# Attention and two feed-forward layers on one core: six weight tiles converted a stage later, the squares' low parts on GpSimd

## The chip, the cores and the metric

The kernel runs on one NeuronCore of a Trainium2 chip. The metric is the time of one execution on the device, in microseconds. Five engines work side by side, each through its own queue in order: TensorE (matmuls, PE in the profile, its weight loads PEld), VectorE (DVE), ScalarE (ACT), GpSimd (POOL) and SyncE (SP), which here issues the DMAs.

## The reference

The input goes through attention with a mask by blocks of 64, and its output, 2304 tokens of 512, through two feed-forward layers of width 2048. The first one squares the positive part of the hidden values, the second one takes a rational function of them.

```python
attn_out = _attn_ref(**attn_kwargs)          # 4 x 8 heads, 576 tokens, 64 wide
x = attn_out.transpose(0, 2, 1, 3).reshape(B * S, H * D)
h = np.maximum(x @ w_in, 0.0)                # first layer, 512 -> 2048 -> 512
x = h * h @ w_out
h = x @ w_in2                                # second layer
P = a[0] + a[1] * h + a[2] * h2 + a[3] * h3
Q = 1.0 + np.abs(b[0]) * np.abs(h) + np.abs(b[1]) * h2
out = P / (Q + 1e-06) @ w_out2
```

## The kernel before, in words

Every product of the feed-forward layers is made of three matmuls: each operand is kept as a high part, rounded to the format of the matmul, and a low part, the rest. PAIRS lists the three combinations.

The weights come in as 64-bit numbers and are converted on the chip, 16 + 16 tiles (in and out) of 128 by 512 for each layer. Converter does that, a job a tile. `load` keeps 2 or 3 raw tiles on the way (SP's queue, L91); a call of `step` finishes the tile before (ScalarE writes its high part at L108, GpSimd its low part at L109) and begins the next one: ScalarE L115, and four instructions of VectorE, L116, L117, L119 and L120. A raw tile's buffer is free for the next load when its L120 is done. Arguments of the call are gates: instructions behind which those of the step are queued on their engine.

The work has three stages.

- Stage one is attention, with the first half (8 of 16 hidden tiles) of the first layer woven in, sequence by sequence (`moe_a`, names ha, ya, ga and s). Its result goes to memory as yp (from yo, L435). The last sequence's share has no attention beside it: the loop at L565 to L573 advances it in 128 pieces and calls convB, which converts the second half's weights (names bi0 to bi7 and bo0 to bo7).
- Stage two is the second half of the first layer (L602 to L645): five blocks of tokens, 384, 384, 512, 512 and 512 wide, 8 units each, one for each hidden tile. A unit u makes h of its tile (12 matmuls, names hb) and y of the tile two units before (12 matmuls, yb). Between the two, `relu_square` takes the positive part (rb, ScalarE), its square's high part (gb, ScalarE L443), the square on VectorE (sb, L444) and its low part (gb, L445). At a block's end VectorE adds yp and stores the sum to xs2. Weights of the second layer (ci0, co0, ci1, ...) are converted beside it by conv3, into buffers of which the later half is free only when stage two has read its own weights for the last time.
- Stage three is the second layer (names hc, yc, gc, t, wq, ab), five blocks of 16 units.

Inputs of a block are read as x (xb, xc), split into high and low by ScalarE and GpSimd (`split_x`). The order in each queue is made by a scheduler that takes the instructions as the program lists them and moves up what it holds to be ready, except behind gates. The numbers in names: ha3_1_7 is sequence 3, part 1, tile 7; hb4_3 is block 4, tile 3.

The lines that the change touches are the two lists of jobs (L559 and L588), the pace of convB (L566), the condition and the place of the call of conv3 in stage two (L612) and the engine of the square's low part (L624):

```python
    def step(self):
        if self.mid:
            ...
            nc.scalar.activation(w[:, 0, :], c, AF.Copy)
            eng.tensor_tensor(w[:, 1, :], c, f(w[:, 0, :]), op=ALU.subtract)
        if self.raws:
            ...
```

Of the kernel before, what the change touches and what calls it, by code (L numbers as in the profile page):

```python
# [24 lines left out]
NM = DFF // P  # L25
HALF = NM // 2
HS = S // 2
SCALE = 0.125
PLAIN = 10
SUBS = ((0, 320), (320, S))  # L30
# [13 lines left out]
def f(ap):  # L44
    return ap.bitcast(F32)
# [3 lines left out]
def attention_moe_moe(ctx: ExitStack, tc: tile.TileContext, q, k, v, wi1, wo1, wi2, wo2, a, b, out):  # L49
    nc = tc.nc  # L50
# [77 lines left out]
    g1 = tc.alloc_tile_pool(name="g1", bufs=1, side="right")  # L128
# [98 lines left out]
    def emit_s(i):  # L227
# [8 lines left out]
        for t in g:  # L236
# [9 lines left out]
            if t == 4:  # L246
                parts = [(ps[:, 0, 0:HS], 0, HS), (ps[:, 1, 0:HS], HS, S)]
            else:
# [191 lines left out]
    def relu_square(alloc, h, g, nm, eng):  # L440
        r, s = alloc("ab", f"r{nm}"), alloc("w", f"s{nm}")
        nc.scalar.activation(r, h, AF.Relu)  # L442
        done = (nc.scalar.activation(g[:, 0, :], r, AF.Square),  # L443
                nc.vector.tensor_tensor(s, r, r, op=ALU.mult))  # L444
        eng.tensor_tensor(g[:, 1, :], s, f(g[:, 0, :]), op=ALU.subtract)  # L445
        return done

    units = [Head(hd) for hd in range(NH_ALL)]
# [43 lines left out]
    for i in range(NI + 5):  # L492
# [22 lines left out]
        for back in range(4):  # L515
            n = units_at.get(i - back)
# [35 lines left out]
    def split_x(xt, kk, n):  # L552
# [3 lines left out]

    w2 = tc.alloc_tile_pool(name="w2", bufs=1, reuse_waits="tile")
    wB = {}
    convB = Converter(g1, 3, [  # L559
        (f"b{kind}{m}", src[HALF + m], w2, kind, wB, m, nc.gpsimd)  # L560
        for m in range(HALF) for kind, src in (("i", wi1), ("o", wo1))])
    n = 0
    SPLITS = (73, 80, 87, 94)
    x_first = load_x(xs, *blocks2[0], "b0")
    while True:  # L565
        if n % 7 == 0:  # L566
            convB()
        if n in SPLITS:
            split_x(x_first, SPLITS.index(n), blocks2[0][1])
        advance(1)  # L570
        if not moes:
            break
        n += 1  # L573
# [7 lines left out]
    g2 = tc.alloc_tile_pool(name="g2", bufs=1, side="right", reuse_waits="tile")  # L581
    psh = tc.alloc_tile_pool(name="psh", bufs=1, space=PSUM, reuse_waits="tile")

    def tmp(tag, n, nm, dt=F32):
        return g2.tile([P, n], dt, tag=tag, name=nm, bufs={"t": 3, "o": 1}.get(tag, 2), padded_shape=[P, 512])

    w3 = {}
    conv3 = Converter(g2, 2, [  # L588
        (f"c{kind}{m}", src[m], wpool if m < HALF else w2, kind, w3, m, nc.gpsimd)
        for m in range(NM) for kind, src in (("i", wi2), ("o", wo2))])  # L590

# [12 lines left out]
    done = ()  # L604
    acc = {}
    units = [(j, m) for j in range(len(blocks2)) for m in range(HALF)]
# [2 lines left out]
    conv3.load()  # L609
    for u in range(len(units) + LAG):  # L610

        if u % 2 == 0 or u > len(units) - HALF:  # L612
            conv3(*done)
        if u < len(units):
            j, m = units[u]
            t0, n = blocks2[j]
            nxt = (xs, *blocks2[j + 1], f"b{j + 1}") if j + 1 < len(blocks2) else (xs2, *blocks3[0], "c0")
            if m == 0:
                xt[j + 1] = load_x(*nxt)
            elif 2 <= m < 2 + KK:  # L620
                split_x(xt[j + 1], m - 2, nxt[2])
            ps = h_matmul(wB["i", m], xt[j], n, f"b{j}_{m}")
            g = g2.tile([P, 2, 512], F32R, tag="g", name=f"gb{j}_{m}", bufs=3)
            done = relu_square(lambda tag, nm: tmp(tag, n, nm), ps[:, 0:n], g[:, :, 0:n], f"b{j}_{m}", nc.vector)  # L624
            gs[u] = g
        if u >= LAG:
            j, m = units[u - LAG]
            t0, n = blocks2[j]
            g = gs.pop(u - LAG)
            last = m == HALF - 1  # L630
            if m == HALF // 2:
                for c in range(KK):
                    ypart[c] = tmp("t" if c < 3 else "o", n, f"yp{j}_{c}")
                    nc.sync.dma_start(ypart[c], yp[:, c, t0:t0 + n])
            for c in range(KK):
                if m == 0:
                    acc[j, c] = psh.tile([P, 512], F32, tag="y", name=f"yb{j}_{c}", bufs=4)
                for i, (zw, zg) in enumerate(PAIRS):
                    nc.tensor.matmul(acc[j, c][:, 0:n], wB["o", m][:, zw, P * c:P * (c + 1)], g[:, zg, 0:n],  # L639
                                     start=m == 0 and i == 0, stop=last and i == 2)  # L640
            if last:
                for c in range(KK):
                    y = ypart[c]
                    nc.vector.tensor_tensor(y, acc.pop((j, c))[:, 0:n], y, op=ALU.add)
                    nc.sync.dma_start(xs2[:, c, t0:t0 + n], y)  # L645


    units = [(j, m) for j in range(len(blocks3)) for m in range(NM)]
    xt = {0: xt[len(blocks2)]}
    mid, gf = {}, {}  # L650
    for u in range(len(units) + LAG):
        if u - 2 in gf:
            t = gf.pop(u - 2)
            n = blocks3[units[u - 2][0]][1]
            g = g2.tile([P, 2, 512], F32R, tag="g", name=f"gc{u - 2}", bufs=3)
# [13 lines left out]
        if u < len(units):  # L669
            j, m = units[u]  # L670
            t0, n = blocks3[j]
# [5 lines left out]
            ps = h_matmul(w3["i", m], xt[j], n, f"c{j}_{m}")  # L677
# [7 lines left out]
            done = (taken, nc.vector.scalar_tensor_tensor(t, t, a1, h, op0=ALU.add, op1=ALU.mult))  # L685
            mid[u] = (ab, w, t)
        if u >= LAG:
            j, m = units[u - LAG]
            t0, n = blocks3[j]
            g = gs.pop(u - LAG)  # L690
            for c in range(n // P):
# [7 lines left out]
                if m == NM - 1:  # L699
                    if c % 2 == 0:  # L700
                        o = g2.tile([P, 2, DM], F32, tag="wraw", name=f"o{j}_{c}", bufs=2)
# [64 lines left out]
```

## Time and profile before

| | |
|---|---|
| median of three runs | 1058.16 us (1053.28 to 1058.83) |
| the profiled execution | 1054.84 us |
| its span | 1053.1 us |
| TensorE busy | 1015.3 us, 96% |
| VectorE busy | 818.8 us, 78% |
| ScalarE busy | 705.8 us, 67% |
| GpSimd busy | 625.3 us, 59% |
| mean granted clock of TensorE | 0.989 |

The profiled execution took 1.74 us more than its span, and lies 3.3 us under the median. Stage one ends at 440.6 us of the span, stage two at 639.9 us. A busy share is a mean over stages: it is read by stretches, and an engine's wait counts where it is the last thing that TensorE waits for.

### The profile page before, as it was taken

The page shows a single profiled execution, that of the slowest core. Times are in us where ns is not written, and L with a number is a line of the kernel's source. Part 1 is how long each engine was busy: PE and PEld are TensorE (multiplying, and loading weights), DVE is VectorE, ACT ScalarE, POOL GpSimd, SP SyncE. Part 2 cuts the span into 40 slices and gives each one's busy share as a digit, 9 for nine tenths or more (in the row PEclk, how much of TensorE's full clock was granted, in tenths as well). Part 3 has the DMA queues.
Part 4 walks back from the last instruction along what each step waited for, and adds up shares of the span by engine and source line. Part 5 has one row for each costly group of instructions (what it writes and reads, how often), then busy time and mean ns, then how long its engine had stood idle before and what let it go on. Part 6 is the DMA issues. An engine that isn't in the chain of part 4 may idle for free.

```text
span 1053.1 us, 17059 instructions
## 1 busy us (share of the span) xinstructions
PE 1015.3 (96%) x5696; PEld 884.6 (84%) x5696; DVE 818.8 (78%) x1584; ACT 705.8 (67%) x1556; POOL 625.3 (59%) x630
## 2 busy tenths in 40 slices
PE   6999899999999998799999999889999999999997
PEld 3667799999999998799888887667888888899996
DVE  7998877878677759978766889888876766776766
ACT  5787677868777754554443445778877777788875
POOL 4789877867686756733321435568555655655542
PEclk9999999999999999899999999999999999999999
DMA  7664433333323215353524355101100200010000
GB/s 249 193 221 144 132 107 105 95 105 117 115 85 107 65 42 165 114 186 122 170 82 139 106 174 163 58 1 41 41 1 1 71 0 1 31 41 1 30 2 30
DMA packets 53784, 96.11 MB, mean 91 GB/s; under 512 B 12096, under 2 KB 27712, under 8 KB 53696
## 3 DMA queue, kind: packets, MB, share of 16 engines
q1 hardware_dynamic: 53408, 94.72, 28.2%
q8 instruction: 45, 0.74, 0.3%
q14 instruction: 43, 0.35, 0.1%
q10 hardware_dynamic: 288, 0.30, 0.1%
HBM read 72.88 MB, written 18.87 MB: 87 GB/s over the span
## 4 chain that ended last, share of the span: by engine, by line
PE 67%; DVE 18%; POOL 4%; ACT 4%; DMA 3%; issue 3%; SPq 0%; POOLq 0%; DVEq 0%; ACTq 0%
PE yc L697 15%; PE hc L597 14%; PE ya L430 7%; PE hb L597 7%; PE ha L418 6%; PE yb L639 6%; PE tp L316 4%; PE pv L382 4%; PE sy L254 2%; DVE stat L277 2%; PE sx L254 2%; DVE s L444 1%; DVE wq L663 1%; DVE gb L445 1%; DMA raw_ci<-in_wi_dram 1%
## 5 line engine op out<-in xcount | busy, mean ns | idle before, releaser
L697 PE MATMUL yc<-w_co,gc 128*128 128x512 f32 x864 | 211.7, 392 | 7.3 <-ACT gc L656 7.3
L597 PE MATMUL hc<-xc,w_ci 128*128 128x512 f32 (+1 forms) x960 | 211.3, 368 | 3.4 <-DVE t L685 3.4
L597 PEld LDWEIGHTS hc<-xc,w_ci 128*128 128x128 f32 x960 | 175.9, 188 | 30.9 <-DVE t L685 4.7
L697 PEld LDWEIGHTS yc<-w_co,gc 128*128 128x128 f32 x864 | 160.7, 188 | 41.6 <-ACT gc L656 10.0
L657 POOL TENSOR_TENSOR gc<-t,gc 128x512 fp32r<-128x512 f32 (+1 forms) x78 | 106.6, 1372 | 134.0 <-issue 91.0
L301 POOL TENSOR_SCALAR p<-p,stat 64x64 f32<-64x64 f32 (+4 forms) x160 | 103.8, 652 | 62.6 <-DVE stat L297 20.2
L430 PE MATMUL ya<-ga,w_ao 128*128 128x320 f32 (+1 forms) x768 | 119.6, 303 | 5.3 <-POOL ga L445 5.1
L418 PE MATMUL ha<-xt,w_ai 128*128 128x320 f32 (+1 forms) x768 | 120.3, 305 | 3.0 <-ACT yo L435 2.4
L430 PEld LDWEIGHTS ya<-ga,w_ao 128*128 128x128 f32 x768 | 108.3, 193 | 7.3 <-POOL ga L445 6.9
L683 POOL TENSOR_TENSOR wq<-wq,ab 128x512 f32<-128x512 f32 (+1 forms) x78 | 96.3, 1235 | 29.6 <-ACT wq L681 29.2
L418 PEld LDWEIGHTS ha<-xt,w_ai 128*128 128x128 f32 x768 | 109.0, 194 | 5.3 <-ACT yo L435 2.6
L597 PE MATMUL hb<-xb,w_bi 128*128 128x512 f32 (+1 forms) x480 | 106.1, 367 | 0.8 <-ACT yo L435 0.8
L639 PE MATMUL yb<-gb,w_bo 128*128 128x512 f32 (+1 forms) x480 | 106.2, 367 | 0.4 <-DVE gb L445 0.4
L684 DVE TENSOR_TENSOR t<-hc,t 128x512 f32<-128x512 f32 (+1 forms) x80 | 50.9, 637 | 63.3 <-ACT t L682 63.3
L656 ACT ACTIVATE gc<-t 128x512 fp32r<-128x512 f32 (+1 forms) x80 | 47.1, 589 | 76.0 <-DVE t L665 74.2
L639 PEld LDWEIGHTS yb<-gb,w_bo 128*128 128x128 f32 x480 | 87.6, 188 | 12.1 <-DVE gb L445 0.7
L597 PEld LDWEIGHTS hb<-xb,w_bi 128*128 128x128 f32 x480 | 87.4, 188 | 12.2 <-ACT yo L435 1.1
L316 PE MATMUL tp<-ident,p 128*128 128x128 f32 (+1 forms) x480 | 84.0, 283 | 4.8 <-POOL p L301 2.7
L348 DVE TENSOR_TENSOR pt<-tp,pt 128x128 fp32r<-128x128 f32 (+2 forms) x176 | 63.2, 391 | 32.7 <-ACT pt L346 22.9
L346 ACT ACTIVATE pt<-tp 128x128 fp32r<-128x128 f32 (+2 forms) x176 | 56.6, 363 | 29.7 <-PE tp L316 27.8
L442 ACT ACTIVATE rb<-hb 128x512 f32<-128x512 f32 (+1 forms) x40 | 22.1, 552 | 80.2 <-PE hb L597 80.2
L663 DVE SCALAR_TENSOR_TENSOR wq<-wq,ab 128x512 f32<-128x512 f32 (+1 forms) x80 | 55.1, 689 | 25.1 <-ACT ab L662 15.8
(120 smaller groups left out, 2092.2 us busy)
## 6 DMA issues: line engine op xcount, KB each, us to landing
qr<-in_q_dram SPq DMA_DIRECT2D x31, 320.0 KB, 3.3
kr<-in_k_dram SPq DMA_DIRECT2D x31, 288.0 KB, 3.6
raw_ci<-in_wi_dram SPq DMA_DIRECT2D x16, 512.0 KB, 3.4
raw_co<-in_wo_dram SPq DMA_DIRECT2D x16, 512.0 KB, 3.7
raw_ai<-in_wi_dram SPq DMA_DIRECT2D x8, 512.0 KB, 4.4
raw_ao<-in_wo_dram SPq DMA_DIRECT2D x8, 512.0 KB, 4.0
raw_bi<-in_wi_dram SPq DMA_DIRECT2D x8, 512.0 KB, 3.5
raw_bo<-in_wo_dram SPq DMA_DIRECT2D x8, 512.0 KB, 3.5
```

The lines of the kernel that those rows point to most:

```text
L301: nc.gpsimd.tensor_scalar(pv, pv, st[r:P, 6 + n:7 + n], 0.0, op0=ALU.mult, op1=ALU.add)
L316: nc.tensor.transpose(ps[:, P * n + r:P * (n + 1)], ptile(slots[i][0], t)[r:P, P * c:P * (c + 1)], ident[r:P, r:P])
L346: nc.scalar.activation(high, src, AF.Copy)
L348: nc.vector.tensor_tensor(low, src, f(high), op=ALU.subtract)
L418: nc.tensor.matmul(ps[:, 0:n], w[:, zw, P * kk:P * (kk + 1)], xt[:, zx, kk, first:end], start=i == 0, stop=i == 3 * KK - 1)
L430: nc.tensor.matmul(ps[:, 0:n], wA["o", m][:, zw, P * c:P * (c + 1)], gs[m][:, zg, 0:n], start=i == 0, stop=i == 3 * HALF - 1)
L597: nc.tensor.matmul(ps[:, 0:n], w[:, zw, P * kk:P * (kk + 1)], xt[:, zx, kk, 0:n], start=i == 0, stop=i == 3 * KK - 1)
L639: nc.tensor.matmul(acc[j, c][:, 0:n], wB["o", m][:, zw, P * c:P * (c + 1)], g[:, zg, 0:n], start=m == 0 and i == 0, stop=last and i == 2)
L657: (nc.vector if u - 2 >= len(units) - END else nc.gpsimd).tensor_tensor(g[:, 1, 0:n], t, f(g[:, 0, 0:n]), op=ALU.subtract)
L663: nc.vector.scalar_tensor_tensor(w, w, Q0, r, op0=ALU.add, op1=ALU.mult)
L683: (nc.vector if u >= len(units) - END else nc.gpsimd).tensor_tensor(w, w, ab, op=ALU.mult)
L697: last = nc.tensor.matmul(acc[j, c], g[:, zg, P * c:P * (c + 1)], w3["o", m][:, zw, :], start=m == 0 and i == 0, stop=m == NM - 1 and i == 2)
```

## The change

convB gets ten of its 16 jobs, called at every tenth piece instead of every seventh. The other six (bi5, bo5, bi6, bo6, bi7, bo7) stand at the head of conv3's list, which then goes on with the second layer's weights. conv3 is called in each of the first 8 units of stage two, as before in every second one up to unit 32, and from unit 33 on at the unit's end, once or twice by turns, so that 35 calls come in stage two instead of 26. The low part of the square in stage two is made by GpSimd.

```diff
+NB = 10
...
-    convB = Converter(g1, 3, [
-        (f"b{kind}{m}", src[HALF + m], w2, kind, wB, m, nc.gpsimd)
-        for m in range(HALF) for kind, src in (("i", wi1), ("o", wo1))])
+    jobsB = [(f"b{kind}{m}", src[HALF + m], w2, kind, wB, m, nc.gpsimd)
+             for m in range(HALF) for kind, src in (("i", wi1), ("o", wo1))]
+
+    convB = Converter(g1, 3, jobsB[:NB])
...
-        if n % 7 == 0:
+        if n % 10 == 0:
             convB()
...
-    conv3 = Converter(g2, 2, [
+    conv3 = Converter(g2, 2, jobsB[NB:] + [
...
-        if u % 2 == 0 or u > len(units) - HALF:
-            conv3(*done)
+
+        before = done
+        if u <= len(units) - HALF and (u % 2 == 0 or u < HALF):
+            conv3(*before)
...
-            done = relu_square(lambda tag, nm: tmp(tag, n, nm), ps[:, 0:n], g[:, :, 0:n], f"b{j}_{m}", nc.vector)
+            done = relu_square(lambda tag, nm: tmp(tag, n, nm), ps[:, 0:n], g[:, :, 0:n], f"b{j}_{m}", nc.gpsimd)
...
+        if u > len(units) - HALF:
+            for _ in range(1 + u % 2):
+                conv3(*before)
```

The changed program's lines behind the first are one higher, and behind stage two's call 4 to 7: L445 there is the square, L446 its low part, and L117, L118, L120 and L121 are the conversion on VectorE.

VectorE's queue at the end of stage one, before (s3_1_k is the square of the last sequence's tile k):

```order
L444 TENSOR_TENSOR s3_1_0_5821<-r3_1_0_5820 128x256
L120 SCALAR_TENSOR_TENSOR cv_bo4_5856<-cv_bo4_5856,raw_bo4_5742 128x512
L444 TENSOR_TENSOR s3_1_1_5841<-r3_1_1_5840 128x256
L116 TENSOR_SCALAR raw_bo5_5814<-raw_bo5_5814 128x512
L117 SCALAR_TENSOR_TENSOR raw_bo5_5814<-raw_bo5_5814 128x512
L119 TENSOR_SCALAR cv_bi5_5906<-cv_bi5_5906 128x512
L444 TENSOR_TENSOR s3_1_2_5872<-r3_1_2_5871 128x256
L120 SCALAR_TENSOR_TENSOR cv_bi5_5906<-cv_bi5_5906,raw_bi5_5778 128x512
L444 TENSOR_TENSOR s3_1_3_5894<-r3_1_3_5893 128x256
L116 TENSOR_SCALAR raw_bi6_5862<-raw_bi6_5862 128x512
L119 TENSOR_SCALAR cv_bo5_5955<-cv_bo5_5955 128x512
L117 SCALAR_TENSOR_TENSOR raw_bi6_5862<-raw_bi6_5862 128x512
```

VectorE's queue in the changed program, from the square of the last sequence's tile 6 on; the squares of the tiles 0 to 5 stand right ahead of it, one behind the other (sb0_0 is the first square of stage two):

```order
L445 TENSOR_TENSOR s3_1_6_5934<-r3_1_6_5933 128x256
L445 TENSOR_TENSOR s3_1_7_5963<-r3_1_7_5962 128x256
L445 TENSOR_TENSOR sb0_0_6135<-rb0_0_6134 128x384
L117 TENSOR_SCALAR raw_bi5_6103<-raw_bi5_6103 128x512
L118 SCALAR_TENSOR_TENSOR raw_bi5_6103<-raw_bi5_6103 128x512
L120 TENSOR_SCALAR cv_bi5_6107<-cv_bi5_6107 128x512
L445 TENSOR_TENSOR sb0_1_6166<-rb0_1_6165 128x384
L117 TENSOR_SCALAR raw_bo5_6105<-raw_bo5_6105 128x512
```

The conversions of bo5 to bo7 and bi5 to bi7 no longer stand between the squares; they follow the first square of stage two.

VectorE's queue in the last block of stage two, before (sb4_3 is the square of tile 3, gb4_3 its low part):

```order
L444 TENSOR_TENSOR sb4_3_7646<-rb4_3_7645 128x512
L116 TENSOR_SCALAR raw_ci10_7578<-raw_ci10_7578 128x512
L117 SCALAR_TENSOR_TENSOR raw_ci10_7578<-raw_ci10_7578 128x512
L445 TENSOR_TENSOR gb4_3_7644<-sb4_3_7646,gb4_3_7644 128x512
L119 TENSOR_SCALAR cv_ci10_7666<-cv_ci10_7666 128x512
L120 SCALAR_TENSOR_TENSOR cv_ci10_7666<-cv_ci10_7666,raw_ci10_7578 128x512
L444 TENSOR_TENSOR sb4_4_7691<-rb4_4_7690 128x512
```

VectorE's queue in the changed program, from the same square to the next one:

```order
L445 TENSOR_TENSOR sb4_3_7624<-rb4_3_7623 128x512
L121 SCALAR_TENSOR_TENSOR cv_ci9_7644<-cv_ci9_7644,raw_ci9_7556 128x512
L118 SCALAR_TENSOR_TENSOR raw_co9_7605<-raw_co9_7605 128x512
L120 TENSOR_SCALAR cv_co9_7655<-cv_co9_7655 128x512
L121 SCALAR_TENSOR_TENSOR cv_co9_7655<-cv_co9_7655,raw_co9_7605 128x512
L117 TENSOR_SCALAR raw_ci10_7650<-raw_ci10_7650 128x512
L118 SCALAR_TENSOR_TENSOR raw_ci10_7650<-raw_ci10_7650 128x512
L120 TENSOR_SCALAR cv_ci10_7700<-cv_ci10_7700 128x512
L445 TENSOR_TENSOR sb4_4_7680<-rb4_4_7679 128x512
```

Between two squares there stood one tile's conversion and a low part; now there stand seven of a conversion's instructions and no low part.

GpSimd's queue in the same block, before:

```order
L109 TENSOR_TENSOR w_ci10_7708<-cv_ci10_7666,w_ci10_7708 128x512
L109 TENSOR_TENSOR w_co10_7753<-cv_co10_7711,w_co10_7753 128x512
L109 TENSOR_TENSOR w_ci11_7804<-cv_ci11_7756,w_ci11_7804 128x512
L109 TENSOR_TENSOR w_co11_7847<-cv_co11_7807,w_co11_7847 128x512
L555 TENSOR_TENSOR xc1_7912<-xc1_7912 128x512 x4
```

GpSimd's queue in the changed program, from the low part of the square of tile 4 on:

```order
L446 TENSOR_TENSOR gb4_4_7678<-sb4_4_7680,gb4_4_7678 128x512
L110 TENSOR_TENSOR w_ci10_7742<-cv_ci10_7700,w_ci10_7742 128x512
L110 TENSOR_TENSOR w_co10_7753<-cv_co10_7745,w_co10_7753 128x512
L446 TENSOR_TENSOR gb4_5_7723<-sb4_5_7725,gb4_5_7723 128x512
L110 TENSOR_TENSOR w_ci11_7804<-cv_ci11_7756,w_ci11_7804 128x512
L446 TENSOR_TENSOR gb4_6_7777<-sb4_6_7779,gb4_6_7777 128x512
L110 TENSOR_TENSOR w_co11_7847<-cv_co11_7807,w_co11_7847 128x512
L110 TENSOR_TENSOR w_ci12_7858<-cv_ci12_7850,w_ci12_7858 128x512
```

The low parts of the squares now stand among those of the weights, one after each one or two.

## Rows read from the trace of the kernel before

**Rows 1.** The page's chain that ended last, by engine, share of the span:

```profile
PE 67%; DVE 18%; POOL 4%; ACT 4%; DMA 3%; issue 3%; SPq 0%; POOLq 0%; DVEq 0%; ACTq 0%
```

**Rows 2.** Windows: stretch, length, busy us (instructions) by engine, PEclk, DMA share, GB/s.

```profile
381.20:440.60 59.40, 51.73 (x352) 49.98 (x351) 54.90 (x65) 33.16 (x69) 42.22 (x35) 0.91 0.37 124
414.30:444.80 30.50, 25.92 (x174) 24.73 (x172) 30.05 (x35) 16.25 (x37) 23.54 (x19) 0.86 0.36 125
428.30:433.00 4.70, 4.69 (x22) 4.69 (x23) 4.67 (x7) 2.42 (x7) 3.77 (x4) 0.52 0.62 219
588.80:633.20 44.40, 44.40 (x197) 36.76 (x197) 39.91 (x52) 21.78 (x37) 18.82 (x12) 1.00 0.48 154
649.80:659.80 10.00, 6.61 (x28) 4.80 (x26) 9.44 (x14) 7.00 (x12) 4.01 (x3) 1.00 0.34 107
659.80:740.00 80.20, 73.92 (x317) 58.72 (x318) 69.56 (x84) 59.98 (x96) 53.37 (x37) 1.00 0.08 27
```

**Rows 3.** TensorE's timeline, end of stage one: start, us, what, [idle before, releaser].

```profile
412.50 9.22 PE L418 MATMUL ha<-xt,w_ai 128*128 128x256 f32 x60 [2.38 <-ACT yo L435]
...
445.75 2.70 PE L597 MATMUL hb<-xb,w_bi 128*128 128x384 f32 x14 [0.79 <-ACT yo L435]
```

**Rows 4.** TensorE's waits from 414 to 441 us: total, times, longest.

```profile
PE ya L430 <- POOL ga L445: 4.4, 3, 3.4
```

**Rows 5.** VectorE's timeline, 577 to 582 us, free and held:

```profile
577.90 0.69 DVE L444 TENSOR_TENSOR sb<-rb 128x512 f32<-128x512 f32 x1 [3.92 <-ACT rb L442]
578.51 0.42 DVE L116 TENSOR_SCALAR raw_co<-raw_co 128x512 uint32<-128x512 uint32 x1
...
579.45 1.79 DVE L117 SCALAR_TENSOR_TENSOR raw_co<-raw_co 128x512 uint32<-128x512 uint32 x1
581.16 0.41 DVE L119 TENSOR_SCALAR cv_co<-cv_co 128x512 f32<-128x512 f32 x1
581.60 0.69 DVE L120 SCALAR_TENSOR_TENSOR cv_co<-cv_co,raw_co 128x512 uint32<-128x512 uint32 x1
```

**Rows 6.** GpSimd's timeline at two places, and one of its groups by shape:

```profile
579.13 1.55 POOL L109 TENSOR_TENSOR w_ci<-cv_ci,w_ci 128x512 fp32r<-128x512 f32 x1 [9.93 <-ACT w_ci L108]
...
621.12 1.35 POOL L109 TENSOR_TENSOR w_ci<-cv_ci,w_ci 128x512 fp32r<-128x512 f32 x1 [1.75 <-ACT w_ci L108]
...
L657 POOL TENSOR_TENSOR gc<-t,gc 128x512 fp32r<-128x512 f32 x48 | 71.8, 1504 | 85.0 <-issue 48.5 <-ACT gc L656 36.5
```

**Rows 7.** VectorE's timeline, last block of stage two and behind it:

```profile
588.78 0.69 DVE L444 TENSOR_TENSOR sb<-rb 128x512 f32<-128x512 f32 x1 [3.92 <-ACT rb L442]
...
616.46 0.43 DVE L116 TENSOR_SCALAR raw_ci<-raw_ci 128x512 uint32<-128x512 uint32 x1 [2.33 <-DMA raw_ci<-in_wi_dram]
...
633.22 0.68 DVE L444 TENSOR_TENSOR sb<-rb 128x512 f32<-128x512 f32 x1
...
634.16 1.78 DVE L445 TENSOR_TENSOR gb<-sb,gb 128x512 fp32r<-128x512 f32 x1
...
643.61 1.87 DVE L644 TENSOR_TENSOR yp<-yb,yp 128x512 f32<-128x512 f32 x3
```

**Rows 8.** TensorE's timeline, from stage two into stage three:

```profile
637.13 2.88 PE L639 MATMUL yb<-gb,w_bo 128*128 128x512 f32 x12
...
659.84 4.91 PE L697 MATMUL yc<-w_co,gc 128*128 128x512 f32 x20 [2.80 <-ACT gc L656]
...
735.23 1.43 PE L597 MATMUL hc<-xc,w_ci 128*128 128x512 f32 x5 [1.70 <-DVE t L685]
```

**Rows 9.** The chain that ended last, in order of time: start, us, what.

```profile
446.14 3.74 DMA raw_ci<-in_wi_dram
...
454.98 2.08 PE hb L597 x12
...
525.55 2.72 PE hb L597 x12
...
610.71 5.73 DMA raw_ci<-in_wi_dram
```

## The prediction

> **What bounds the kernel now.** I read the chain that ended last first: TensorE holds 67% of it, VectorE 18% [rows 1]. So TensorE is the rule and VectorE the exception, and the question is where the exception lies. The windows by stretch answer it: from 381.2 to 440.6 us TensorE is busy 51.73 of 59.40 us, from 649.8 to 659.8 us 6.61 of 10.00, from 659.8 to 740 us 73.92 of 80.20 [rows 2]. Elsewhere it hardly waits. In all three stretches VectorE converts weight tiles. In the first of them its stretch from 414.3 to 444.8 us is full, 30.05 of 30.50 us [rows 2].
>
> The third reading is why VectorE is full. Its instructions are short when GpSimd rests: 0.42, 0.69, 0.41 and 0.69 us for the four of a conversion, 0.69 us for a square [rows 5]. Each starts 0.08 us before the end of the one ahead (578.51 + 0.42 is 578.93, the next starts at 578.84), so a tile costs 1.9 us and a square 0.61. But L117 at 579.45, which meets a GpSimd instruction that began at 579.13 and ends at 580.68, takes 1.79 us and ends at 581.24 [rows 5, 6]: it stood until GpSimd had done. The window 588.8 to 633.2 us, the last block of the second stage, gives the mean price. VectorE is busy 39.91 us with 52 instructions; 8 tiles at 1.9, 16 products and subtractions at 0.61 and 4 additions at 0.6 (three take 1.87 us beside GpSimd, which doesn't hold them, [rows 7]) make 27.4. The other 12.5 us fall to 12 GpSimd instructions, **1.04 us each** [rows 2]. So work that goes from VectorE to GpSimd doesn't leave VectorE: it saves 0.61 us and costs 1.04 while VectorE has anything to do.
>
> **The change part by part.**
>
> *Six tiles leave the end of the first stage.* The order of VectorE is the same up to the last instruction of cv_bi4, which runs in the trace just behind TensorE's wait at 412.50; from there the eight products s3_1_0 to s3_1_7 follow each other without a conversion between them. What stands before stays: also that wait, 2.38 us for a bank [rows 3]. What goes are the three waits for ga behind it, 4.4 us [rows 4], and the clock that fell with the last of them: from 428.3 to 433.0 us the granted clock was 0.52 of 2.4 GHz, nearly all of it at 1.2, with TensorE busy 4.69 us, so 4.69 x 0.48 = 2.25 us [rows 2]. The 0.79 us wait of hb for a late eviction at 445.75 goes too [rows 3]. What is late next: GpSimd does w_bi4 and w_bo4 ahead of its eight ga and should hand over the last of them 0.7 us late (0 to 1.5). Sum **-6.7 us** (-7.4 to -5.9).
>
> *They come back in block 0 of the second stage.* T0 is the block's first matmul. A run of 12 matmuls of 384 columns takes 2.08 us [rows 9], and y of unit 7 is the 18th run, due at T0 + 35.4. The load of raw_bi5 stands on SP's queue behind the four stores of yo, the last of which comes some 1 us after T0; with 3.74 us for a load [rows 9] (the order of the stores and the 1 us are an estimate from where the store of the last yo stands) the first conversion starts at T0 + 4.7. Until product sb0_7 VectorE has 8 tiles at 1.9 and 7 products at 0.47 (0.61 less the quarter of the columns), 18.5 us; GpSimd has 7 low parts of weights at 1.04 and 7 of squares at 0.8, 12.9 us. That ends at T0 + 36.1, the last gb 1.1 us later: 1.8 us late. The nearest weights, w_bi7, come out about as late for h7. I take **+2 us** (0, if GpSimd works in VectorE's gaps, to 5, if each load of a raw tile is waited for, since there are two).
>
> *Low parts of the squares on GpSimd, blocks 1 to 3.* One tile in two units, a unit two runs of 2.08 or 2.72 us [rows 9]: VectorE needs 0.6 + 0.95 and GpSimd 1.3 + 0.7. TensorE is never late there now and isn't then: **0**. Without that cover each gb would cost what GpSimd's form takes over VectorE's, 1.50 against 0.69 us [rows 5, 6]; and g has two whole units until its y.
>
> *The last block.* Before, 8 tiles stand between sb3_7 (588.78) and sb4_7 (633.22) [rows 7]; after, 12, as the order shows, and 24 GpSimd instructions (8 gb, 12 low parts of weights, 4 of xc0) in place of 12. VectorE: 12 x 1.9 + 8 x 0.61 + 2.4 = 30.1 us; GpSimd 24 x 1.04 = 25.0; idle, mostly for loads behind the stores of yp (L116 at 616.46 waited 2.33 us for one, and its load had taken 5.73 us), 44.40 - 39.91 = 4.5 as before [rows 2, 7, 9]. Sum 59.6 against 44.4: sb4_7 comes **15 us later**. Low end 11, if GpSimd's work fills the idle 4.5; high end 18, because a third conversion in two units leaves a raw tile no time: a load of 3.74 us [rows 9] starts only when the tile two places ahead is done. I take 15, nearest to the window that the price comes from. Before, y of unit 7 was hardly delayed (gb4_7 ended at 634.16 + 1.78 = 635.9, TensorE began it at 637.13, [rows 7, 8]): that slack of 1 us is gone at once.
>
> *From there to the third stage's first y*, 633.22 to 659.84 us before, 26.6 us [rows 7, 8], VectorE leads: TensorE needs 6 x 2.72 = 16.3 us for six h [rows 9] and then waits 2.80 [rows 8]. After, the order has one instruction more ahead of t0, two more behind it and one more low part on GpSimd: +1.5 (0 to 2). First y **16.5 us later** (11 to 20). This holds the waits of TensorE in the last block and is not to be added to them.
>
> *What the third stage saves.* After that y, before has four tiles left (ci14, co14, ci15, co15), after one. TensorE idles 80.20 - 73.92 = 6.28 us there [rows 2], of which 1.70 at 735.23 follow the splits of xc2, not a tile [rows 8]. Three quarters of the other 4.6 go: **-3.5** (-4.7 to 0).
>
> Sum: -6.7 + 2 + 0 + 16.5 - 3.5 = **+8.3 us**. The profiled execution took 1054.84 us, so 1063; the runs' median is 3.3 us above it, and on that scale it is 1058.16 + 8.3 = 1066.5, rounded to **1066**. Ends of the terms together: about 0 to +16, 1058 to 1074.
>
> A rule weighed. Rows 5 and 6 show an instruction held until GpSimd's ended, and the window a mean of 1.04 us. The Trainium skill, SBUF — State Buffer, "Who interferes with whom", says that the port pair that VectorE and GpSimd share is an exclusive lock held for the whole instruction, so the second "fully blocks". By that a GpSimd instruction beside a full VectorE costs its whole 1.35 us [rows 6], and 12 more of them 3.7 us more than by the window: +12 in place of +8.3. The window decides; the rule speaks against this change and against the faster rival.
>
> **The rivals.**
>
> *Faster: the last block keeps up.* GpSimd's added work falls into the 4.5 us in which VectorE idles and into the additions of yp. For it: the products' results are wanted two units later, and VectorE loses its 8 subtractions. Against it: two more tiles a block end alone are 4 x 1.9 = 7.6 us, and the stretch is 90% full. It decides at a growth of the stretch of 6.7 + 3.5 - 2 - 1.5 = 6.7 us: below that the kernel gains. With no growth: -6.7 + 0 + 0 - 3.5 = -10, 1048.
>
> *No difference: half of it.* The stretch grows by 6 to 9 us, since loads and locks overlap better than in the window: -6.7 + 2 + 9 - 3.5 = +1, 1059. The row for it is GpSimd's idle time (18.82 of 44.40 us busy, [rows 2]).
>
> *Much slower.* The loads are waited for at each tile (+20) and the clock falls in the last block's waits, as it did after the 3.4 us wait [rows 4] (2.25 us): +16, 1074.
>
> *The change isn't carried out as told*: the scheduler could have left the conversions where they were. The order of the changed program shows them moved; no chance.
>
> **How the numbers follow.** Forecast 0.48, no difference 0.26, faster 0.18, much slower 0.08. A measurement of this kernel tells about 0.5%, 5.3 us, from no change. Slower by more: 0.48 + 0.08 = 0.56; within: 0.26; faster: 0.18. The range goes down to 1050, which leaves out the better part of the faster case, some 0.13, and up to 1076, which leaves out 0.05.
>
> **What would show it.** Right: ya of the last sub-block without a wait and without a clock fall after it; TensorE waiting for gb from GpSimd in the last block, in all over 8 us; the first yc some 28 us after sb4_7; gaps of under 2 us behind it until 740. VectorE's mean for the conversions' instructions up in the last block. Wrong: no wait for gb there, or sb4_7 less than 7 us later after the block's first matmul than the 42.5 of before; a stall of over 5 us in block 0; or a clock that stays at 1.2 GHz over the last block.

## The result and the profile after

The changed kernel takes 1067.95 us in the median of four runs (1066.63 to 1071.88), the kernel before 1056.93 us beside it (1053.28 to 1058.83, four runs). The ratio is 1.0117, with a 95% interval of 1.0097 to 1.0137: 12.4 us longer (10.3 to 14.5). The prediction was +8.3 us, 1066, in a range of 1050 to 1076.

The profiled execution took 1071.88 us, with a span of 1070.1. It is cut here at events that both kernels have: TensorE's wait for yo at the end of stage one, the first matmul of stage two, of block 1, of block 1's fifth unit, of the last block, and of the third stage's first y. All are starts in TensorE's timeline.

| stretch | before, us | after, us | difference | predicted |
|---|---|---|---|---|
| start to the end of the wait for yo | 412.50 | 416.44 | +3.94 | 0 |
| to stage two | 28.13 | 21.78 | -6.35 | -5.9 |
| block 0 | 30.82 | 31.05 | +0.23 | +1.2 |
| block 1, four units | 16.64 | 22.99 | +6.35 | 0 |
| to the last block | 102.58 | 102.57 | 0 | 0 |
| last block, to the third stage's first y | 69.17 | 88.04 | +18.87 | +16.5 |
| from there to the end | 393.26 | 387.23 | -6.03 | -3.5 |

(The prediction's -6.7 held 0.79 us of a wait that lies behind the first matmul of stage two; it is moved to block 0 here.) The first row is for the most part not the change: the profiles of nine kernels below with the same first stage end that wait at 411.64 to 414.76 us, so this execution was 2 to 5 us late before anything that the change touches, as its time, 3.9 us over the median, says too. The other rows sum to +13.1 us.

The page's busy line of the changed kernel, and its chain that ended last, by engine, where TensorE has 66% in place of 67 and DMA 6% in place of 3 [rows 1]:

```profile
PE 1022.5 (96%) x5696; PEld 888.7 (83%) x5696; DVE 793.6 (74%) x1544; ACT 706.6 (66%) x1556; POOL 669.4 (63%) x670
...
PE 66%; DVE 17%; DMA 6%; ACT 5%; POOL 3%; issue 3%; SPq 0%; POOLq 0%; DVEq 0%; ACTq 0%
```

TensorE's timeline of the changed kernel (start, us, what, idle before and releaser) at the cuts and the large waits:

```profile
416.44 7.52 PE L419 MATMUL ha<-xt,w_ai 128*128 128x256 f32 x48 [2.84 <-ACT yo L436]
...
425.68 12.70 PE L431 MATMUL ya<-ga,w_ao 128*128 128x256 f32 x96
438.22 6.75 PE L599 MATMUL hb<-xb,w_bi 128*128 128x384 f32 x38
...
469.27 2.24 PE L599 MATMUL hb<-xb,w_bi 128*128 128x384 f32 x12
...
482.17 0.59 PE L643 MATMUL yb<-gb,w_bo 128*128 128x384 f32 x2 [1.25 <-DVE yp L648]
485.12 0.69 PE L643 MATMUL yb<-gb,w_bo 128*128 128x384 f32 x1 [2.37 <-POOL gb L446]
...
492.26 2.24 PE L599 MATMUL hb<-xb,w_bi 128*128 128x384 f32 x12
...
594.83 2.88 PE L599 MATMUL hb<-xb,w_bi 128*128 128x512 f32 x12
...
648.24 4.14 PE L643 MATMUL yb<-gb,w_bo 128*128 128x512 f32 x10 [2.12 <-POOL gb L446]
...
674.20 8.23 PE L599 MATMUL hc<-xc,w_ci 128*128 128x512 f32 x24 [6.13 <-DVE t L692]
682.87 4.89 PE L704 MATMUL yc<-w_co,gc 128*128 128x512 f32 x20 [0.44 <-ACT gc L663]
```

And its windows (length, busy us by engine, granted clock, DMA share, GB/s): block 1's first four units, the part of them in which the clock was low, the last block from sb3_7 to sb4_7, and the stretch ahead of the first y:

```profile
469.27:492.26 22.99, 19.16 (x98) 17.99 (x98) 19.61 (x26) 11.07 (x22) 16.30 (x13) 0.93 0.56 180
485.10:490.20 5.10, 5.08 (x21) 5.08 (x22) 5.07 (x8) 0.14 (x1) 4.22 (x3) 0.68 0.56 169
593.00:652.90 59.90, 52.17 (x214) 40.24 (x212) 48.10 (x61) 25.95 (x45) 34.16 (x24) 0.97 0.44 142
674.20:682.00 7.80, 7.80 (x23) 6.20 (x24) 7.73 (x11) 4.18 (x7) 3.13 (x3) 0.66 0.21 68
```

The first rows answer to [rows 3, 4]: the wait for yo is still there (2.84 us, 2.38 before), but the 12.70 us of y from 425.68 on run through, and stage two starts at their end. The 4.4 us of waits for ga are gone, and the granted clock over these 12.70 us is 1.00. What came is in two places. In block 1 TensorE waits 1.25 us for a bank and 2.37 us for gb, idles 3.83 of the 22.99 us, and then has a granted clock of 0.68 from 485.1 to 490.2 us, two thirds of it at 1.2 GHz and the rest at 2.4. In the last block it waits for gb again, and behind the block 6.13 us for t; from there the clock is 0.66 up to the first y. That fall of the clock cost nothing: the y still waited 0.44 us for its operand (2.80 before, [rows 8]). From 405 to 1045 us TensorE's three largest waits are (total, times, longest):

```profile
PE yb L643 <- POOL gb L446: 8.7, 7, 2.4
PE hc L599 <- DVE t L692: 6.1, 1, 6.1
PE yb L643 <- DVE yp L648: 3.0, 3, 1.3
```

### The profile page after: what moved, and what is told of

The parts are those of the page before. It is cut to its first block, busy times and chain, and to the rows that moved or that the text cites. A ratio compares the mean times of both kernels' runs of the same rounds, so it can differ in the third digit from the quotient of the medians.

```text
span 1070.1 us, 17092 instructions
## 1 busy us (share of the span) xinstructions
PE 1022.5 (96%) x5696; PEld 888.7 (83%) x5696; DVE 793.6 (74%) x1544; ACT 706.6 (66%) x1556; POOL 669.4 (63%) x670
## 3 DMA queue, kind: packets, MB, share of 16 engines
HBM read 72.88 MB, written 18.87 MB: 86 GB/s over the span
## 4 chain that ended last, share of the span: by engine, by line
PE 66%; DVE 17%; DMA 6%; ACT 5%; POOL 3%; issue 3%; SPq 0%; POOLq 0%; DVEq 0%; ACTq 0%
PE yc L704 14%; PE hc L599 14%; PE ya L431 8%; PE ha L419 7%; PE hb L599 5%; PE yb L643 5%; PE tp L317 4%; PE pv L383 4%; PE sy L255 3%; PE sx L255 2%; DMA raw_ci<-in_wi_dram 2%; DVE wq L670 1%; DVE t L672 1%; DVE stat L278 1%; DMA raw_bi<-in_wi_dram 1%
## 5 line engine op out<-in xcount | busy, mean ns | idle before, releaser
L599 PE MATMUL hc<-xc,w_ci 128*128 128x512 f32 (+1 forms) x960 | 213.6, 371 | 6.1 <-DVE t L692 6.1
L643 PE MATMUL yb<-gb,w_bo 128*128 128x512 f32 (+1 forms) x480 | 111.6, 377 | 12.9 <-POOL gb L446 8.7
L446 POOL TENSOR_TENSOR gb<-sb,gb 128x512 fp32r<-128x512 f32 (+1 forms) x40 | 51.1, 1277 | 77.2 <-DVE sb L445 73.5
L599 PEld LDWEIGHTS hb<-xb,w_bi 128*128 128x128 f32 x480 | 88.2, 189 | 12.7 <-POOL w_bi L110 1.5
```

The lines of the kernel that those rows point to most:

```text
L599: nc.tensor.matmul(ps[:, 0:n], w[:, zw, P * kk:P * (kk + 1)], xt[:, zx, kk, 0:n], start=i == 0, stop=i == 3 * KK - 1)
```

## Where block 1 loses its time

Block 1 was forecast at nothing. The queue of the DMAs shows why it is not. These are SP's issues (start, us, what) at the start of block 1, of the kernel before and of the changed one; xb is the x of block 2, whose buffer comes free with block 0's last h:

```profile
466.13 0.33 SPq L91 DMA_DIRECT2D raw_co<-in_wo_dram  x1
469.57 1.75 SPq L549 DMA_DIRECT2D xb<-xs  x4
```

```profile
470.42 0.33 SPq L92 DMA_DIRECT2D raw_ci<-in_wi_dram  x1
474.80 0.33 SPq L92 DMA_DIRECT2D raw_co<-in_wo_dram  x1
475.18 1.85 SPq L550 DMA_DIRECT2D xb<-xs  x4
```

Before, xb was issued 1.9 us ahead of block 1's first matmul (471.45). After, the raw_co in front of it waits longer for its buffer (the tile two places ahead is converted later), and xb is issued 5.9 us behind that matmul (469.27). The timelines of ScalarE, GpSimd and VectorE in the changed kernel show who pays:

```profile
478.94 0.64 ACT L555 ACTIVATE xb<-xb 128x512 fp32r<-128x512 f32 x1 [2.97 <-DMA xb<-xs]
```

```profile
479.65 4.15 POOL L556 TENSOR_TENSOR xb<-xb 128x512 fp32r<-128x512 f32 x3 [1.55 <-ACT xb L555]
483.76 1.31 POOL L446 TENSOR_TENSOR gb<-sb,gb 128x384 fp32r<-128x384 f32 x1
```

```profile
480.88 0.56 DVE L445 TENSOR_TENSOR sb<-rb 128x384 f32<-128x384 f32 x1 [1.76 <-ACT rb L443]
481.47 0.56 DVE L648 TENSOR_TENSOR yp<-yb,yp 128x384 f32<-128x384 f32 x1
```

ScalarE stands 2.97 us at the first split of xb, with the rb of block 1's first tile behind it (480.37). VectorE waits for that rb, and the addition of yp, which frees TensorE's bank, stands behind its square. GpSimd makes three splits (4.15 us) before the same tile's gb, which begins at 483.76 and ends at 485.07; TensorE takes it at 485.12. Whether it is this load, or simply too much work in block 0, was put to an experiment (split_later).

## Experiments

The numbers of all runs stand together, each as the difference to the kernel before (us, from the profiles, cut as above, blocks 0 and 1 up to the fifth unit in one; from there to the last block no kernel differs by more than 0.1). The last column is the ratio of the times with its interval.

| kernel | to stage two | block 0 and four units | last block to first y | behind it | ratio |
|---|---|---|---|---|---|
| changed | -6.4 | +6.6 | +18.9 | -6.0 | 1.0117 (1.0097 to 1.0137) |
| gb_alone | 0.0 | +0.8 | +1.1 | -0.2 | 1.0011 (1.0000 to 1.0022) |
| gb_back | -6.4 | +3.0 | +11.9 | -6.1 | 1.0010 (0.9993 to 1.0027) |
| last_back | -6.2 | +6.6 | +0.3 | +5.3 | 1.0059 (1.0040 to 1.0078) |
| split_later | -6.4 | +0.8 | +18.3 | -6.0 | 1.0058 (1.0041 to 1.0075) |
| move_alone | -6.3 | +3.7 | -2.1 | +6.6 | 1.0019 (1.0001 to 1.0037) |
| light_last | -6.3 | +6.9 | +8.2 | -7.3 | 1.0024 (1.0010 to 1.0038) |
| light_load | -6.3 | +6.6 | +12.1 | -6.1 | 1.0065 (1.0042 to 1.0088) |
| light_both | -6.2 | +6.7 | +5.2 | -6.0 | 0.9998 (0.9984 to 1.0012) |
| combined | -6.3 | -0.7 | -0.1 | -0.3 | 0.9936 (0.9918 to 0.9953) |
| combined_yp | -6.4 | -0.6 | +1.4 | -4.1 | 0.9920 (0.9900 to 0.9940) |

**split_later.** The splits of block 2's x go two units back, each behind a gate:

```diff
-            elif 2 <= m < 2 + KK:
-                split_x(xt[j + 1], m - 2, nxt[2])
+            elif 2 + 2 * (j == 1) <= m < 2 + 2 * (j == 1) + KK:
+                with tc.issue_after(done[0].ins) if j == 1 else ExitStack():
+                    split_x(xt[j + 1], m - 2 - 2 * (j == 1), nxt[2])
```

> The changed kernel with the four splits of block 2's x two units later in block 1, each behind the square's high part of the unit before. No load, no conversion and no low part is moved. Theory: block 1 loses its time because the load of that x stands on SP's queue behind a raw tile's load that waits for its buffer (issued 475.2 us against 469.6 before), and ScalarE and GpSimd stand at the splits with rb and gb behind them; with the splits later block 1's first four units take 16.6 to 18 us instead of 23.0, 5 to 6 us less in all, 1062 to 1063. Rival: block 0's conversions overload VectorE and GpSimd and the lateness runs over into block 1; then the 23.0 us stay, and so does 1068.

Its xb is issued as late as in the changed kernel (470.72 us, behind a raw_co, 5.6 us after block 1's first matmul at 465.08), but rb and gb no longer stand behind its splits. TensorE's waits from 434 to 500 us:

```profile
PE hb L599 <- POOL w_bi L110: 1.2, 1, 1.2
PE yb L644 <- POOL gb L446: 0.2, 1, 0.2
```

The waits for gb go from 2.7 us to 0.2, the stretch from +6.6 to +0.8, and the kernel from 1.0117 to 1.0058. The theory holds: it was the place of the splits of a late x in two queues that work in order, not the amount of work. The 1.2 us for w_bi that stay are those that the prediction had for block 0.

**gb_alone** and **gb_back.** The low part alone, and everything but the low part:

```diff
 # gb_alone, against the kernel before
-            done = relu_square(..., f"b{j}_{m}", nc.vector)
+            done = relu_square(..., f"b{j}_{m}", nc.gpsimd)
 # gb_back, against the changed kernel
-            done = relu_square(..., f"b{j}_{m}", nc.gpsimd)
+            done = relu_square(..., f"b{j}_{m}", nc.vector)
```

> The kernel before with the square's low part in stage two on GpSimd, nothing else changed. Theory: in blocks 0 to 3 it is covered, since the x of the next block comes early there (its loads are issued at 469.6 us of the span before, 5.6 us earlier than in the changed kernel), so block 1 keeps its 16.6 us; in the last block eight instructions of 0.61 us leave VectorE and each of GpSimd's holds it for 0.75 to 1.04 us, so sb4_7 comes 1 to 3.5 us later; in all +1 to +4 us, 1058 to 1061. Rival: the low parts alone are what costs; then block 1 is 4 us or more longer here too and the whole is +8 us or more.

> The changed kernel with the square's low part back on VectorE. Theory: the loss in block 1 (from its first matmul to that of its unit 4, 23.0 us against 16.6 before) falls to 3 us or so, because the low parts no longer stand behind the four splits of x on GpSimd, while ScalarE still holds rb for the late x; the last block's stretch is 1 to 4 us shorter; in all 4 to 7 us less than the changed kernel, 1061 to 1064. Rival: VectorE is the bound in both places, and takes the low parts back at 0.61 us each: no change against the changed kernel, 1068.

gb_alone came at the low end of the theory's range (+0.11%, 1 us; sb4_7 0.8 us later, where 1 to 3.5 were expected). gb_back fell by more than expected, to the time of the kernel before: 3.6 us in block 1 and 7.0 us in the last block. The same eight low parts cost 1.1 us where the last block has eight tiles and 7.0 us where it has twelve. (The pair last_back and move_alone below, also with one tile for each unit, differs by 2.4 us there.) The windows from the last block's first matmul to sb4_7, of gb_alone and of gb_back, say what differs:

```profile
591.07:634.40 43.33, 43.33 (x193) 35.85 (x192) 40.72 (x43) 20.31 (x34) 29.66 (x20) 1.00 0.48 150
```

```profile
587.90:640.65 52.75, 48.77 (x206) 39.14 (x204) 47.20 (x65) 24.73 (x41) 21.87 (x16) 0.97 0.47 152
```

With eight tiles the stretch lasts 43.33 us, and TensorE is busy in all of it: what GpSimd takes from VectorE (busy 40.72 us, 38.04 before) is hidden up to there. With twelve tiles TensorE idles 4 of 52.75 us even with the low parts on VectorE; there the block goes at the pace of the conversions, and what GpSimd takes is seen. The rival of gb_back, that VectorE takes its work back at no gain, falls with it; only the size in the last block, 7.0 us where 1 to 4 were expected, was beyond the theory.

**last_back** and **move_alone.** The last block as before, with the low part on GpSimd and on VectorE:

```diff
-        if u <= len(units) - HALF and (u % 2 == 0 or u < HALF):
+        if u % 2 == 0 or u < HALF or u > len(units) - HALF:
...
-        if u > len(units) - HALF:
-            for _ in range(1 + u % 2):
-                conv3(*before)
 # move_alone also
-            done = relu_square(..., f"b{j}_{m}", nc.gpsimd)
+            done = relu_square(..., f"b{j}_{m}", nc.vector)
```

> The changed kernel with the last block's calls as before (one for each unit, at the unit's start; 30 calls in stage two instead of 35). Theory: the last block's four additional tiles are what makes its stretch to the third stage's first y 18.9 us longer; without them it is 3 to 6 us longer than before, but eight tiles are left for stage three, where each costs about 1 to 1.5 us: the 6 us that stage three gained go, and 2 us more. In all 5 to 8 us less than the changed kernel, 1060 to 1063. Rival: tiles converted early are worth their price; then this kernel is as slow as the changed one or slower, 1068 to 1072.

> The kernel before with the six tiles moved alone: the square's low part stays on VectorE and the last block has one tile for each unit, as before (30 calls in stage two for 38 tiles). Theory, from the terms that the runs so far showed one by one: -6.4 us at the end of stage one, +3.0 us from the first matmul of stage two to block 1's unit 4 (with the low parts on VectorE), 0 in the last block and up to the third stage's first y, +5.2 us behind it for the two tiles more that are left for stage three. In all +1 to +2.5 us, 1057 to 1059. Rival: the terms don't add, since the last block begins with two tiles more to do and VectorE is full there: +6 us or more.

Both times came as the theories have them (1061.29 and 1057.84 us), but last_back's by two errors that cancel: its stretch to the first y is 0.3 us longer than before, not 3 to 6, and what follows loses 11.3 us against the changed kernel, not 8. In move_alone the last block is 2.1 us shorter and what follows 1.4 us longer than the terms. These two give the price of a tile. Behind the first y VectorE begins one tile in the changed kernel and in gb_back, six in last_back and move_alone (four before). With the low part on GpSimd five tiles cost 18.9 - 0.3 = 18.6 us ahead of the first y, 3.7 us each, and save 5.3 + 6.0 = 11.3 us behind it, 2.3 us each. With the low part on VectorE they cost 14.0 us, 2.8 each, and save 12.7, 2.5 each. So tiles brought forward into the last block are at a clear loss with GpSimd's additional work (ratio 1.0117 against 1.0059). Without it the profiles differ by 1.3 us, and the times show no loss: 1.0010 for gb_back, 1.0019 for move_alone, with intervals that overlap.

**light_last, light_load, light_both.** What the last block's twelve tiles cost it: VectorE's instructions, or the loads? The first cuts VectorE's columns to an eighth, the second the loads, the third both:

```diff
 # light_last
+                k = 64 if job[0][0] == "c" and HALF <= int(job[0][2:]) < 14 else 512
+                low, high, c0, cu = low[:, 0:k], high[:, 0:k], c[:, 0:k], cu[:, 0:k]
 # light_load
-                nc.sync.dma_start(raw.rearrange("p n t -> p (n t)"), job[1])
+                n = 64 if light else 512
+                nc.sync.dma_start(raw[:, 0:n].rearrange("p n t -> p (n t)"), job[1][:, 0:2 * n])
```

> The changed kernel with VectorE's four instructions of the conversion on an eighth of the columns for the tiles ci8 to co13 (12 tiles, those of the last block); seven eighths of these tiles' values are left unconverted, so the output isn't the reference's. All loads, ScalarE's and GpSimd's work and the order stay. Theory: the last block is long because VectorE is full, with GpSimd's instructions holding it; with some 1.6 us less of VectorE for each tile the product sb4_7 comes 43 to 47 us after the block's first matmul instead of 58, and the third stage's first y 10 to 16 us earlier. Rival: it is the raw tiles' loads, two buffers with 3.7 us or more for each load and 11.8 us of idle time on VectorE in the trace; then sb4_7 stays at 54 us or later.

> The changed kernel with an eighth of each raw tile loaded (64 KB in place of 512) for ci8 to co13, the 12 tiles of the last block; ScalarE and VectorE work on 448 or 512 columns as before, read from the 64 that were loaded, so the output isn't the reference's; the scheduler places a few instructions otherwise. In light_last, with VectorE's work taken away and the loads kept, sb4_7 came 50.2 us after the block's first matmul (58.0 in the changed kernel, 42.5 before), and VectorE waited 12.9 us for loads. Theory now: both chains cost, a load of 3.7 us or more between two uses of a raw buffer and VectorE with GpSimd's locks, so that with short loads sb4_7 comes 50 to 54 us after the first matmul. Rival: the loads only fill what VectorE leaves idle; with VectorE at its full work they cost nothing, and sb4_7 stays at 56 to 58 us.

> light_load and light_last together: an eighth of the loads and an eighth of VectorE's columns for the same 12 tiles; ScalarE's and GpSimd's work stays; the output isn't the reference's. Theory: VectorE's work and the loads are the only two causes, so that the block runs at TensorE's pace: sb4_7 42 to 44.5 us after the first matmul and no wait of y for gb. Rival: a third one is there (ScalarE's or GpSimd's order, the stores of yp, the banks), and sb4_7 comes 46 us after it or later.

From the block's first matmul to sb4_7 it is 58.0 us in the changed kernel, 42.5 before, and 50.2, 52.3 and 46.5 in these three. In light_last VectorE is busy 32.6 of the 50.2 us, where it was 46.3 of 58.0, and the block gains 7.8 (the first y comes 10.7 us earlier); its waits from 588 to 650 us show what takes over, 12.9 us for raw tiles (the scheduler placed a few instructions otherwise here too, which the expectation did not say):

```profile
DVE raw_ci L119 <- DMA raw_ci<-in_wi_dram: 7.9, 5, 3.6
...
DVE raw_co L119 <- DMA raw_co<-in_wo_dram: 5.0, 3, 2.9
```

50.2 us lies between the first run's theory and its rival. In light_load the waits for raw tiles are 4.9 us, and the block is 5.7 us shorter, as its theory has it. So neither VectorE nor the loads alone explain it: they bound the block by turns, and taking one away brings the other up. In the third run TensorE doesn't wait for gb any more, as the theory said, but the block falls to the rival: 46.5 us is 2 us above the theory's range, and VectorE now waits 7.3 us for ScalarE's first step of a tile (cv). The longest of these waits, 2.84 us, ends with a cv at 618.08, for which ScalarE had itself waited 0.88 us for GpSimd's low part of an earlier tile. Of the 18.9 us ahead of the first y, 13.7 go with both; the other 5.2 were not taken apart.

**combined** and **combined_yp.** The six tiles moved, the low part on VectorE, the splits as in split_later, the last block as before, and two tiles more in blocks 2 and 3, so that the last block begins with as many done as before:

```diff
-        if u <= len(units) - HALF and (u % 2 == 0 or u < HALF):
+        if u % 2 == 0 or u < HALF or u in (19, 27) or u > len(units) - HALF:
 # combined_yp instead, with the last two calls behind the additions of yp
+        if u % 2 == 0 or u < HALF or u in (19, 27) or len(units) - HALF < u < len(units):
...
+    for _ in range(LAG):
+        conv3(added)
```

> The six tiles moved as in the changed kernel, the low part on VectorE, the splits of block 2's x two units later, two additional tiles in blocks 2 and 3 (units 19 and 27), where TensorE never waits, and the last block as before, which so begins and ends with the same tiles as in the kernel before. Theory: -6.4 us at the end of stage one, up to +1 us in block 0, nothing elsewhere: -5 to -6 us against the kernel before, 1050 to 1052. Rival: the move is a loan that has to be paid somewhere (the two additional tiles and the late x turn up as waits in blocks 2 and 3 or in the last one): no difference to the kernel before, 1055 to 1058.

> As the kernel 'combined', with the last two calls of stage two behind the four additions of yp on VectorE instead of ahead of them. In the kernel before the additions began at 643.6 us, 3.7 us after TensorE's last matmul of their sums, behind two tiles' conversions, and the third stage's t waits for the store that follows them. Theory: the additions come 3 us earlier and the third stage's first y 1 to 3 us, of which the tiles, later by a place, take back 0 to 2: 0 to -3 us against 'combined', 1048 to 1051. Rival: VectorE is full up to the first y anyway, and the order of its work there makes no difference: 0 to +2 us.

combined takes 1048.83 us beside 1055.08 us of the kernel before, 0.64% less and a little more than the theory's 5 to 6 us: the 6.3 us at the end of stage one are kept and nothing is paid back. TensorE's waits in combined, from 405 us to the end, have no y in stage two:

```profile
PE yc L702 <- ACT gc L661: 6.0, 5, 2.8
PE hc L599 <- DVE t L690: 3.3, 3, 1.7
PE ha L419 <- ACT yo L436: 2.8, 1, 2.8
PE hb L599 <- POOL w_bi L110: 0.7, 1, 0.7
```

combined_yp takes 1046.50 us, 0.80% less than before and 2.3 us less than combined (their intervals overlap), as far as the theory said, but not by its way: the additions came 4.6 us earlier behind the block's first matmul (they begin at 632.79 against 637.65 us of the span), and the first y 1.4 us later, not earlier. VectorE's queue holds two tiles between t and wq there (645.77 and 648.20 us) where combined has one (647.27), so one tile less, three in place of four, is left behind the first y, and 3.8 us go there. What the additions gained was lost again: t's first step came at 642.07 us without an idle moment of VectorE ahead of it, behind the conversions that the additions had passed.

## Why the prediction was right, and where it was not

The direction and its cause were right: the end of stage one gains, and the last block loses more. That the time came within 2 us of 1066 is in part luck: one stretch forecast at nothing lost 6.35 us, others came out better than their terms, and the kernel before had a median 1.2 us lower beside it. (The ends of the prediction's terms add up to -1.1 and +19.1 us, and not to "about 0 to +16".)

**The end of stage one** was right: -6.35 against -5.9 for this stretch, with the waits and the clock's fall gone as the trace had priced them, and it shows in every kernel with the tiles moved (-6.2 to -6.4).

**Block 0** was right in its kind: 1.22 us for w_bi7 and two waits of 0.2 us for gb, the second of them already in block 1, against the forecast 2.

**Blocks 1 to 3 at nothing** is the step that failed. It set VectorE's and GpSimd's times for a tile against a unit, and did not follow the queue that issues the loads. A raw tile's load stands ahead of the load of the next x in both kernels; with a call in each unit it waits longer for its buffer, and x with it, and the splits of that x stand early in ScalarE's and GpSimd's order. That is +6.35 us: 3.83 of idle TensorE, some 1.6 of the lower clock (5.08 us at 0.68), the rest not taken apart. split_later gives back 5.8. "Without that cover each gb would cost ..." named the right engine, but for the wrong reason: gb stood behind the splits.

**The last block** was right in its sum, and for partly wrong reasons. sb4_7 came 15.5 us later (forecast 15). But VectorE is busy 48.10 of the 59.9 us, not 55: 12 tiles at 1.9, eight products at 0.61 and four additions make 30.1, so that the 24 GpSimd instructions took 18.0 us, 0.75 us each and not 1.04. And it idles 11.8 us, not 4.5, of which 9.9 are loads. The largest wait for a load, in VectorE's timeline and in the chain that ended last:

```profile
616.23 0.68 DVE L445 TENSOR_TENSOR sb<-rb 128x512 f32<-128x512 f32 x1
623.44 0.43 DVE L117 TENSOR_SCALAR raw_ci<-raw_ci 128x512 uint32<-128x512 uint32 x1 [6.52 <-DMA raw_ci<-in_wi_dram]
```

```profile
616.78 6.56 DMA raw_ci<-in_wi_dram
```

The last conversion out of raw_ci's buffer ends only at 615.72 us; the load is issued at 616.78, behind a load of yp, and takes 6.56 us. The prediction had this as an end of its range ("a third conversion in two units leaves a raw tile no time") and as a half of the much slower rival; light_load, in which the loads of all twelve tiles are short, shows them worth some 5.7 us. TensorE's waits for gb in this block are 6.0 us, where the prediction's sign was over 8.

**From sb4_7 to the first y** came 3.4 us later, not 1.5. The sums' last matmul ends at 657.4 us, the additions begin at 665.14, behind two tiles, and t's first step waits 3.33 us on ScalarE for their store:

```profile
665.14 1.87 DVE L648 TENSOR_TENSOR yp<-yb,yp 128x512 f32<-128x512 f32 x3
```

```profile
670.31 0.78 ACT L689 ACTIVATE t<-hc,coef 128x512 f32<-128x512 f32 x1 [3.33 <-DMA xs<-yp]
```

Before, the additions began 3.6 us after the last matmul [rows 7, 8]; now 7.7. This was priced as one instruction more; the trace shows two tiles in front of the additions. That they are the cause was argued and not shown: in combined_yp the additions came earlier, and the first y did not.

**Stage three** saved 6.0 and not 3.5. TensorE's idle time behind the first y fell by 4.7 us; the 1.70 us at 735.23 [rows 8], which the prediction left standing as the splits', are not there after. The other 1.4 us are busy time, and their cause stays open (over the last 153.1 us TensorE is busy 147.17 us before and 147.29 after, so it is not the clock at the end).

**The rule weighed.** By the Trainium skill (SBUF — State Buffer, "Who interferes with whom") the shared port is an exclusive lock for a whole instruction, which would have made +12 of the sum. The measured +12.4 is no support for it: 6.35 of it lie in block 1, and GpSimd's 24 instructions took 34.16 us in the last block's window and cost VectorE 18.0. A single instruction of VectorE that meets one of GpSimd's does stand until that ends (the last section has one); but others of GpSimd's fall into VectorE's waits and cost nothing: 3.65 us of GpSimd's work lie in the wait of 6.52 us shown above.

So the forecast of +8.3 fell short of the rows' +13.1 by what block 1 lost, 6.35 us, and 2.4 us in the last stretch, less the 2.5 us that stage three saved beyond its term and 1.4 us in the first two stretches; the first of these is the only one of another kind than was forecast.

## What to carry over

Work that is moved into an idle stretch of one engine takes its loads with it: look at what stands behind them in the queue that issues them, and at which in-order queue waits for that. A price per piece is read on both sides of a move (here 3.7 us for a tile ahead and 2.3 behind with the low part on GpSimd, 2.8 and 2.5 with it on VectorE, and nothing in the blocks where TensorE never waits), and pieces go where it is lowest. Work given to a helper whose instructions hold up those of the busy engine is nearly free only while that one has slack: the same eight instructions cost 1.1 to 2.4 us with eight tiles begun in the block and 7.0 with twelve.

## What was not expected of the hardware

An instruction of VectorE on 64 columns that meets GpSimd is held as one on 512 is. In light_last the same step takes 0.23 us free and 1.24 us while GpSimd works from 617.55 to 618.85 us (VectorE's timeline, then GpSimd's):

```profile
616.47 0.23 DVE L120 SCALAR_TENSOR_TENSOR raw_ci<-raw_ci 128x64 uint32<-128x64 uint32 x1
...
617.70 1.24 DVE L120 SCALAR_TENSOR_TENSOR raw_co<-raw_co 128x64 uint32<-128x64 uint32 x1
```

```profile
617.55 1.30 POOL L110 TENSOR_TENSOR w_co<-cv_co,w_co 128x512 fp32r<-128x512 f32 x1 [3.45 <-ACT w_co L109]
```

And a load of 64 KB was not an eighth of one of 512: in light_load a raw tile was issued at 619.92 and used at 621.85 us, 1.9 us, against 3.4 to 6.6 us for the whole tiles of the changed kernel's chain. By the Trainium skill (DMA: Bandwidth & Descriptors, "Anatomy of one DMA — SWDGE (gpsimd) path") a transfer issued from GpSimd has a fixed part of about 2.0 us; this load is issued from SyncE, so no run here tests that figure.
